# A mixture of experts on one Trainium2 core: the experts' second product with stationary weights and 512 moving tokens

## Chip, core and metric

The kernel runs on one core of one Trainium2 chip. The metric is the device time of one execution in microseconds (us), as the median of several executions. All operands are float32 in memory.

## What is computed

The program runs three stages one after the other, each on the output of the stage before. Cut to what matters:

```python
def _attn_ref(r, k, v, w, u):          # 2 batches, 8 heads, 768 tokens, 48 dimensions
    ...
    for t in range(S):
        cur = np.einsum('bhd,bhe->bhde', u[None] * kt, vt)
        y[:, :, t] = np.einsum('bhd,bhde->bhe', rt, state + cur)
        state = wt[:, :, :, None] * state + np.einsum('bhd,bhe->bhde', kt, vt)

def _moe_ref(x, w_in, w_out):          # x: 1536 x 384, inner width 2048
    h = x @ w_in
    return (h * np.clip(h + 3.0, 0.0, 6.0) / 6.0) @ w_out

def _moe2_ref(x, w_gate, w1, w2):      # 8 experts, inner width 1024
    logits = x @ w_gate
    P = np.exp(logits - logits.max())
    for _ in range(8):
        P /= P.sum(1, keepdims=True) + 1e-09
        P /= P.sum(0, keepdims=True) + 1e-09
        P *= N / E
    out = np.zeros((N, D))
    for e in range(E):
        out += P[:, e:e + 1] * (np.maximum(x @ w1[e], 0.0) @ w2[e])
    return out
```

So every token goes through every expert, and the routing weight P of a token and an expert is one factor on that expert's whole output row.

## The kernel before

Float32 accuracy is kept by splitting each operand of a product into a high and a low part (type fp32r): `parts_of` (line 110) makes `wah`, `wal` and `wbh`, `wbl` of the weights. Each product is then three matmuls: high with high, high with low, low with high.

The program is a list of units, written out in `fast` (line 641). A unit has an upper half (first product and activation) and a lower half (second product), and the lower half runs two units later (`LAG = 2`). Tables of jobs, keyed by unit, put everything else (loads, splits, the routing's normalisation, the input test) between the halves. From the first lower half of the experts on, the order is exactly the order in which the code is written (`manual_schedule`, line 782). Before it, in the first two stages, a scheduler chooses.

The experts are 192 units, one for each expert e (8), block m of 512 tokens (3) and slice f of 128 inner columns (8).

- `ex_up` (line 398): nine matmuls with 128x128 of the expert's first weights as the stationary operand and 512 tokens of `x2h` or `x2l` as the moving one, all into one PSUM tile `ph`. ScalarE makes `hh` (line 410) and VectorE `hl` (line 411), the high and low part of the activated slice: 128 inner columns by 512 tokens.
- `ex_down` (line 414): the second product with the tokens' slice stationary. For each of the 4 groups of 128 tokens, three matmuls: 128x128 of `hh` or `hl` stationary, 384 columns of `wbh` or `wbl` moving, into a PSUM tile `y0` to `y3` of 128 tokens by 384 dimensions, summed over the eight slices f. After slice 7 (a block's end), the sum goes into `acc`, 128 tokens by 384 dimensions each: for expert 0 as a plain copy on ScalarE (line 430), since the routing weights are not ready then. For expert 1 VectorE multiplies `acc` by expert 0's weight (line 433). From expert 1 on it adds `y` times the weight of this expert (line 434). There the weight is one number for each partition, since tokens lie on partitions. After expert 7, `acc` is stored (line 438).
- `acc` lies in the memory of `x2f` (line 540), six tiles of 128 dimensions by 3 by 256 tokens, whose contents are no longer wanted by then.

The four `y` tiles have one buffer each: the first matmul of the next block into `y0` waits until `y0` was read out. PSUM holds 2 tiles `ph`, 4 tiles `y` and 1 for small things (`pss`), of 8 banks.

VectorE executes in the order written: between the `hl` of each unit stand the splits of the next expert's weights (line 114, two 128x768 subtractions every fourth unit), the normalisation of the routing (units 2 to 24 of the experts) and the input test (`flag_stages`, line 441), whose steps load a piece of the inputs into `seen` and look at it. All loads are issued on SyncE's queue (SP) in the order written.

The lines that the prediction's steps touch: matmuls of the first product of the experts L406, of the second L424; their evacuations L410, L411, L430, L433, L434; first and second product of the stage before L274 and L296, where L296 already has weights stationary and 256 tokens moving; transposes on TensorE L253; the subtraction L310 over 128x768 and L283 over 128x256.

Of the kernel before, what the change touches and what calls it, by code (L numbers as in the profile page):

```python
# [8 lines left out]
F32 = mybir.dt.float32  # L9
# [3 lines left out]
AF = mybir.ActivationFunctionType  # L13
ALU = mybir.AluOpType
AX = mybir.AxisListType
PSUM = bass.MemoryType.PSUM

B, H, S, D = 2, 8, 768, 48
DM = H * D
N = B * S  # L20
E = 8
F1 = 2048
FE = 1024
C = 128
NC = S // C
# [18 lines left out]
class Kernel:  # L44
# [269 lines left out]
    def sinkhorn_stages(self):  # L314
# [5 lines left out]
        def gate():  # L320
            gf = pp.tile([128, KT, E], F32, tag="gf", name="gf")
            nc.sync.dma_start(out=gf, in_=self.w_gate.rearrange("(k p) e -> p k e", p=128))
            zero = pp.tile([128, KT, E], F32, tag="gz", name="gz")
            nc.vector.memset(zero, 0.0)
            g = pp.tile([128, KT, 2 * E], F32R, tag="gt", name="gt")
            hi, lo = g[:, :, :E], g[:, :, E:]
            nc.vector.tensor_copy(hi, gf)
            nc.vector.tensor_tensor(out=lo, in0=gf, in1=hi.bitcast(F32), op=ALU.subtract)
            g0 = pp.tile([128, KT, 2 * E], F32R, tag="g0", name="g0")
            nc.vector.tensor_copy(g0[:, :, :E], gf)  # L330
            nc.vector.tensor_copy(g0[:, :, E:], zero)
            q["g"] = g, g0
            q["lt"] = pp.tile([2 * E, N], F32, tag="lt", name="lt")

        def logits(m):
            def go():
# [75 lines left out]
        self.h[e, m, f] = (hh, hl)  # L412

    def ex_down(self, e, m, f):
        nc = self.nc
        bh, bl = self.down_parts(2 + e, f)
        hh, hl = self.h.pop((e, m, f))
        if f == 0:
            self.y = [self.psy.tile([128, 512], F32, tag=f"y{i}", name=f"y{i}") for i in range(4)]
        for i in range(4):  # L420
            o = self.y[i][:, :DM]
            sl = slice(i * 128, (i + 1) * 128)
            for n, (ha, wb) in enumerate(((hh, bh), (hh, bl), (hl, bh))):
                nc.tensor.matmul(o, ha[:, sl], wb, start=f == 0 and n == 0, stop=f == 7 and n == 2)  # L424
        if f == 7:
            for i in range(4):
                t = 4 * m + i
                o, acc = self.y[i][:, :DM], self.acc[t]
                if e == 0:
                    nc.scalar.activation(acc, o, AF.Copy)  # L430
                    continue
                if e == 1:
                    nc.vector.tensor_scalar(out=acc, in0=acc, scalar1=self.pr[:, t, 0:1], scalar2=None, op0=ALU.mult)  # L433
                nc.vector.scalar_tensor_tensor(out=acc, in0=o, scalar=self.pr[:, t, e:e + 1], in1=acc,  # L434
                                               op0=ALU.mult, op1=ALU.add)
                if e == E - 1:
                    c, b = t // 2, t % 2
                    nc.sync.dma_start(out=self.out[b * S + c * C:b * S + (c + 1) * C, :], in_=acc)


    def flag_stages(self):
# [74 lines left out]
    def pool(self, es, name, bufs=1, **kw):  # L516
        return es.enter_context(self.tc.tile_pool(name=name, bufs=bufs, **kw))
# [25 lines left out]
    def slow(self):  # L543
        tc, nc, pool = self.tc, self.nc, self.pool
        self.general = True
        with ExitStack() as top:
            dram = pool(top, "dram", space=bass.MemoryType.DRAM)
            y = dram.tile([DM, B, S], F32, name="y")
            with ExitStack() as es:
                p, q = pool(es, "sa"), pool(es, "sb", 2)  # L550
                ps = pool(es, "sps", 2, space=PSUM)
# [69 lines left out]
            self.hp = pool(top, "hp", 4)  # L621
            self.psy = pool(top, "psy", space=PSUM)
            self.p2 = pool(top, "p2")
            self.pss = pool(top, "pss", space=PSUM)
            self.pr = self.p2.tile([128, N // 128, E], F32, tag="pr", name="pr")
            for st in self.sinkhorn_stages():
                st()
            for e in range(E):
                for i in range(NCH):
                    self.load_chunk(NCH * e + i)  # L630
                    self.split_chunk(NCH * e + i, nc.vector)
                self.lagged([(self.ex_up, self.ex_down, (e, m, f)) for m in range(3) for f in range(8)])

    def lagged(self, units):
        for n in range(len(units) + LAG):
# [5 lines left out]
    def fast(self):  # L641
        tc, nc, pool = self.tc, self.nc, self.pool
        self.general = False
        with ExitStack() as top:
            self.pools(top)
            keep = self.keep
            ph1, ph1x, ph1a = ExitStack(), ExitStack(), ExitStack()
            self.p1 = _Bufs(pool(ph1, "p1", side="right"), {"gh": 3, "gl": 3, "t": 2})
# [40 lines left out]
            def at(n, fn, *args):  # L689
                jobs.setdefault(int(2 * n + 1), []).append((fn, args))  # L690
# [68 lines left out]
            def second():  # L759
                self.x2_parts(NC - 1)  # L760
                ph1.close()
                self.p2 = pool(top, "p2")
                self.pss = pool(top, "pss", space=PSUM)
                self.pr = self.p2.tile([128, N // 128, E], F32, tag="pr", name="pr")
                self.sk = self.sinkhorn_stages()
                self.accumulators()
            at(n1 + LAG - 1, second)
            for s in range(7 + 2 * SK_ITERS):
                at(n1 + LAG + s, lambda s: self.sk[s](), s)

            def flag(x):
                if x == 0:
                    self.fl = self.flag_stages()
                self.fl[x]()
            nst = 2 + 4 * NC * B + 4 * F1 // CH
            lo, hi = n1 + 24, len(units) - 30
            for x in range(nst):
                at(lo + x * (hi - lo) // nst, flag, x)

# [73 lines left out]
```

## Time and profile before

| | |
|---|---|
| median of 3 runs | 1149.19 us (1148.93 to 1149.87) |
| the profiled execution, its own time | 1148.96 us |
| its span in the trace (first to last instruction) | 1147.0 us |
| mean granted TensorE clock | 0.98 of full speed |
| TensorE busy (matmul, weight load) | 97%, 89% of the span |
| VectorE, ScalarE, GpSimd busy | 51%, 28%, 5% |
| DMA traffic | 77.64 MB, mean 68 GB/s |

The profile page gives busy time by engine, the span in 40 slices, the chain of work that ended last, and groups of instructions by line. PE is TensorE's matmul, PEld its weight load, DVE is VectorE, ACT ScalarE, POOL GpSimd and SP SyncE's queue. In the timeline each row is an instruction with its start, its duration, and behind `[` the idle time before it. A matmul's shown duration reaches into the next one's, as matmuls are pipelined: what one costs is read from the start of one to the start of the next.

The experts' part begins at 326 us of the span and ends 6 us before its end.

### The profile page before, as it was taken

The page shows a single profiled execution, that of the slowest core. Times are in us where ns is not written, and L with a number is a line of the kernel's source. Part 1 is how long each engine was busy: PE and PEld are TensorE (multiplying, and loading weights), DVE is VectorE, ACT ScalarE, POOL GpSimd, SP SyncE. Part 2 cuts the span into 40 slices and gives each one's busy share as a digit, 9 for nine tenths or more (in the row PEclk, how much of TensorE's full clock was granted, in tenths as well). Part 3 has the DMA queues.
Part 4 walks back from the last instruction along what each step waited for, and adds up shares of the span by engine and source line. Part 5 has one row for each costly group of instructions (what it writes and reads, how often), then busy time and mean ns, then how long its engine had stood idle before and what let it go on. Part 6 is the DMA issues. An engine that isn't in the chain of part 4 may idle for free.

```text
span 1147.0 us, 15722 instructions
## 1 busy us (share of the span) xinstructions
PE 1112.6 (97%) x6471; PEld 1020.4 (89%) x6471; DVE 583.2 (51%) x1121; ACT 325.7 (28%) x672; POOL 62.4 (5%) x57
## 2 busy tenths in 40 slices
PE   7789989999999999999999999999999999999998
PEld 6678889999998999998999999999999999989997
DVE  8799694535633442554354445345445544532221
ACT  3555554445622222221121122112112211211111
POOL 3443220000000000000000000000000000000000
PEclk7698999999999999999999999999999999999999
DMA  9455330100111001201210220122142124100000
GB/s 293 145 168 183 105 131 2 37 11 1 56 56 36 29 1 44 79 25 52 79 53 25 79 80 25 52 80 89 52 151 74 54 79 137 56 1 1 28 28 31
DMA packets 44208, 77.64 MB, mean 68 GB/s; under 512 B 3296, under 2 KB 26976, under 8 KB 44128
## 3 DMA queue, kind: packets, MB, share of 16 engines
q1 hardware_dynamic: 44128, 76.55, 21.4%
q8 instruction: 53, 0.87, 0.3%
q14 instruction: 27, 0.22, 0.1%
HBM read 74.18 MB, written 2.36 MB: 67 GB/s over the span
## 4 chain that ended last, share of the span: by engine, by line
PE 86%; DVE 9%; DMA 2%; POOL 1%; ACT 1%; issue 1%; SPq 0%; ACTq 0%; DVEq 0%; POOLq 0%
PE y L424 35%; PE ph L406 35%; PE ph L274 7%; PE xa L296 4%; PE xb L296 2%; DMA rkt<-in_tm_dram 1%; DVE x L70 1%; DVE x L71 1%; DVE e L152 1%; DVE gl L283 1%; DVE f L159 1%; PE y L223 1%; DVE x L69 1%; DVE t L279 1%; DMA v<-in_tm_dram 1%
## 5 line engine op out<-in xcount | busy, mean ns | idle before, releaser
L411 DVE SCALAR_TENSOR_TENSOR hl<-ph,hh 128x512 fp32r<-128x512 f32 x192 | 132.7, 691 | 431.0 <-ACT hh L410 430.9
L410 ACT ACTIVATE hh<-ph 128x512 fp32r<-128x512 f32 x192 | 114.6, 597 | 642.9 <-PE ph L406 642.9
L424 PE MATMUL y<-wbh,hl 128*128 128x384 f32 x768 | 259.1, 337 | 0.0
L424 PE MATMUL y<-wbh,hh 128*128 128x384 f32 x768 | 259.0, 337 | 0.0
L424 PE MATMUL y<-wbl,hh 128*128 128x384 f32 x768 | 257.9, 336 | 0.0
L406 PE MATMUL ph<-x2h,wal 128*128 128x512 f32 x576 | 227.8, 396 | 0.0
L406 PE MATMUL ph<-x2l,wah 128*128 128x512 f32 x576 | 227.2, 394 | 0.0
L406 PE MATMUL ph<-x2h,wah 128*128 128x512 f32 x576 | 225.2, 391 | 0.9 <-DVE off L505 0.9
L424 PEld LDWEIGHTS y<-wbh,hh 128*128 128x128 f32 x768 | 144.3, 188 | 8.9 <-DVE x2f L434 0.5
L424 PEld LDWEIGHTS y<-wbl,hh 128*128 128x128 f32 x768 | 144.2, 188 | 8.3
L424 PEld LDWEIGHTS y<-wbh,hl 128*128 128x128 f32 x768 | 144.0, 188 | 0.0
L406 PEld LDWEIGHTS ph<-x2h,wal 128*128 128x128 f32 x576 | 108.0, 187 | 23.3
L406 PEld LDWEIGHTS ph<-x2h,wah 128*128 128x128 f32 x576 | 108.3, 188 | 18.5 <-DVE off L505 0.9
L406 PEld LDWEIGHTS ph<-x2l,wah 128*128 128x128 f32 x576 | 108.1, 188 | 18.2
L274 PE MATMUL ph<-x1h,wah 128*128 128x256 f32 x288 | 84.8, 295 | 3.7 <-DVE t L279 3.7
L274 PE MATMUL ph<-x1h,wal 128*128 128x256 f32 x288 | 81.3, 284 | 1.7 <-DVE wal L114 1.7
L274 PE MATMUL ph<-x1l,wah 128*128 128x256 f32 x288 | 81.9, 285 | 0.0
L277 ACT ACTIVATE t<-ph,three 128x256 f32<-128x256 f32 x96 | 44.5, 470 | 65.1 <-PE ph L274 56.9
L279 DVE SCALAR_TENSOR_TENSOR t<-t,ph 128x256 f32<-128x256 f32 x96 | 39.5, 416 | 44.5 <-ACT t L277 44.4
L296 PE MATMUL xa<-gl,wbh 128*128 128x256 f32 x192 | 56.0, 292 | 6.1 <-DVE gl L283 6.1
L274 PEld LDWEIGHTS ph<-x1h,wah 128*128 128x128 f32 x288 | 55.5, 193 | 6.1 <-DVE t L279 5.1
L274 PEld LDWEIGHTS ph<-x1h,wal 128*128 128x128 f32 x288 | 54.9, 191 | 2.1 <-DVE wal L114 2.1
(125 smaller groups left out, 1309.8 us busy)
## 6 DMA issues: line engine op xcount, KB each, us to landing
stg<-in_w_dram SPq DMA_DIRECT2D x64, 384.0 KB, 4.7
stg<-in_w_in_dram SPq DMA_DIRECT2D x8, 768.0 KB, 6.4
stg<-in_w_out_dram SPq DMA_DIRECT2D x8, 768.0 KB, 4.7
seen<-in_w_in_dram SPq DMA_DIRECT2D x8, 768.0 KB, 4.8
seen<-in_w_out_dram SPq DMA_DIRECT2D x8, 768.0 KB, 4.4
rk<-in_dm_dram SPq DMA_DIRECT2D x12, 448.0 KB, 3.9
seen<-in_dm_dram SPq DMA_DIRECT2D x12, 448.0 KB, 3.8
rkt<-in_tm_dram SPq DMA_DIRECT2D x12, 384.0 KB, 3.9
```

Source lines behind the costliest of these rows:

```text
L69: nc.vector.tensor_scalar(out=x, in0=high, scalar1=3, scalar2=0x3FFFFFF8, op0=ALU.logical_shift_left, op1=ALU.bitwise_and)
L70: nc.vector.scalar_tensor_tensor(out=x, in0=high, scalar=0xC0000000, in1=x, op0=ALU.bitwise_and, op1=ALU.bitwise_or)
L71: nc.vector.scalar_tensor_tensor(out=x, in0=low, scalar=29, in1=x, op0=ALU.logical_shift_right, op1=ALU.bitwise_or)
L152: nc.vector.tensor_tensor_scan(out=e.rearrange("p i t -> p (i t)"), data0=w[:, :WCOL - 1], data1=self.d1e.rearrange("p i t -> p (i t)"), i ...
L274: nc.tensor.matmul(ph, wa[:, kt, :], xa[:, kt, :], start=n == 0, stop=n == 3 * KT - 1)
L277: nc.scalar.activation(t, ph, AF.Relu, bias=self.three)
L279: self.last_u = nc.vector.scalar_tensor_tensor(out=u, in0=t, scalar=6.0, in1=ph, op0=ALU.min, op1=ALU.mult)
L296: nc.tensor.matmul(o, wb[:, kt * 128:(kt + 1) * 128], ga, start=start and n == 0 and kt != 1, stop=stop and n == 2, skip_group_check=True)
L406: nc.tensor.matmul(ph, wa[:, kt, :], xa[:, kt, sl], start=n == 0, stop=n == 3 * KT - 1)
L410: nc.scalar.activation(hh, ph, AF.Relu)
L411: nc.vector.scalar_tensor_tensor(out=hl, in0=ph, scalar=0.0, in1=hh.bitcast(F32), op0=ALU.max, op1=ALU.subtract)
L424: nc.tensor.matmul(o, ha[:, sl], wb, start=f == 0 and n == 0, stop=f == 7 and n == 2)
```

## The change

`ex_down` is turned round for all blocks but the last (expert 7, block 2). For each of three groups of 128 model dimensions, `wbh` or `wbl` (128x128) is stationary and the 512 tokens of `hh` or `hl` move, into `y0`, `y1` and `y2`, each 128 dimensions by 512 tokens. The sums are kept by model dimension, in `x2f`'s own layout (`accumulate`). A routing weight is now one number for each column, so the weights have to stand as a row, the same on all 128 partitions: `keep_routing` transposes the finished `pr` and writes it to DRAM (`pd`), and `spread_routing` loads one expert's 1536 weights onto all partitions (`pb`, 128x1536). `weigh_first` multiplies expert 0's sums by its weights. From expert 1 on, VectorE multiplies `y` by `pb` into `p` (128x512) and adds the two halves of `p` to the two tiles of `x2f`.

The output wants tokens on partitions: `turn` transposes one chunk of 256 tokens back (six 128x128 transposes on TensorE, two copies on ScalarE into `acc`), and `store` writes it. Chunks 4 and 5 are turned during expert 7's first block, before the last block, which still works by token, adds to them. Chunks 0 to 3 are finished and stored while the last block runs. `pss` gets a second buffer, so that all 8 PSUM banks are in use. The input test starts 12 units later (36 instead of 24 units into the experts) and ends at the same unit.

The diff, without the slow path that runs only if the input test fails, and without line changes that follow from it:

```diff
@@ -412,30 +412,86 @@
         self.h[e, m, f] = (hh, hl)
 
     def ex_down(self, e, m, f):
         nc = self.nc
         bh, bl = self.down_parts(2 + e, f)
         hh, hl = self.h.pop((e, m, f))
+        by_token = (e, m) == (E - 1, 2)
         if f == 0:
-            self.y = [self.psy.tile([128, 512], F32, tag=f"y{i}", name=f"y{i}") for i in range(4)]
-        for i in range(4):
-            o = self.y[i][:, :DM]
+            self.y = [self.psy.tile([128, 512], F32, tag=f"y{i}", name=f"y{i}") for i in range(4 if by_token else KT)]
+        for i, y in enumerate(self.y):
             sl = slice(i * 128, (i + 1) * 128)
-            for n, (ha, wb) in enumerate(((hh, bh), (hh, bl), (hl, bh))):
-                nc.tensor.matmul(o, ha[:, sl], wb, start=f == 0 and n == 0, stop=f == 7 and n == 2)
+            for n, (wb, ha) in enumerate(((bh, hh), (bl, hh), (bh, hl))):
+                go = dict(start=f == 0 and n == 0, stop=f == 7 and n == 2)
+                if by_token:
+                    nc.tensor.matmul(y[:, :DM], ha[:, sl], wb, **go)
+                else:
+                    nc.tensor.matmul(y, wb[:, sl], ha, **go)
         if f == 7:
-            for i in range(4):
-                t = 4 * m + i
-                o, acc = self.y[i][:, :DM], self.acc[t]
-                if e == 0:
-                    nc.scalar.activation(acc, o, AF.Copy)
-                    continue
-                if e == 1:
-                    nc.vector.tensor_scalar(out=acc, in0=acc, scalar1=self.pr[:, t, 0:1], scalar2=None, op0=ALU.mult)
-                nc.vector.scalar_tensor_tensor(out=acc, in0=o, scalar=self.pr[:, t, e:e + 1], in1=acc,
-                                               op0=ALU.mult, op1=ALU.add)
-                if e == E - 1:
-                    c, b = t // 2, t % 2
-                    nc.sync.dma_start(out=self.out[b * S + c * C:b * S + (c + 1) * C, :], in_=acc)
+            for i, y in enumerate(self.y):
+                if by_token:
+                    t = 4 * m + i
+                    nc.vector.scalar_tensor_tensor(out=self.acc[t], in0=y[:, :DM], scalar=self.pr[:, t, e:e + 1],
+                                                   in1=self.acc[t], op0=ALU.mult, op1=ALU.add)
+                    self.store(t)
+                else:
+                    self.accumulate(e, m, i, y)
+    def accumulate(self, e, m, i, y):
+        nc = self.nc
+        halves = [(self.x2f[2 * m + s][:, i, :], slice(s * NB1, (s + 1) * NB1)) for s in range(2)]
+        if e == 0:
+            for x, s in halves:
+                nc.scalar.activation(x, y[:, s], AF.Copy)
+            return
+        p = self.tmp.tile([128, KT * CH], F32, tag="x", name="p")[:, :512]
+        nc.vector.tensor_tensor(out=p, in0=y, in1=self.pb[:, m * 512:(m + 1) * 512], op=ALU.mult)
+        for x, s in halves:
+            nc.vector.tensor_tensor(out=x, in0=x, in1=p[:, s], op=ALU.add)
+    def store(self, t):
+        c, b = t // 2, t % 2
+        self.nc.sync.dma_start(out=self.out[b * S + c * C:b * S + (c + 1) * C, :], in_=self.acc[t])
+    def keep_routing(self):
+        nc, pp = self.nc, self.p2
+        NT = N // 128
+        pe = pp.tile([128, E, NT], F32, tag="lg", name="pe")
+        nc.vector.tensor_copy(pe, self.pr.rearrange("p t e -> p e t"))
+        ps = self.pss.tile([E * NT, 128], F32, tag="s", name="pt")
+        nc.tensor.transpose(ps, pe.rearrange("p e t -> p (e t)"), self.ident)
+        pt = pp.tile([128, N], F32, tag="lt", name="pt")[:E * NT, :128]
+        nc.vector.tensor_copy(pt, ps)
+        nc.sync.dma_start(out=self.pd, in_=pt)
+    def spread_routing(self, e):
+        tag = "lt" if e else "seen"
+        self.pb = self.p2.tile([128, N], F32, tag=tag, name="pb")
+        row = self.pd.rearrange("(e t) p -> e (t p)", e=E)[e:e + 1, :]
+        self.nc.sync.dma_start(out=self.pb, in_=row.to_broadcast([128, N]))
+    def weigh_first(self, c, pb):
+        x = self.x2f[c]
+        w = pb[:, c * NB1:(c + 1) * NB1].unsqueeze(1).to_broadcast([128, KT, NB1])
+        self.nc.vector.tensor_tensor(out=x, in0=x, in1=w, op=ALU.mult)
+    def turn(self, c):
+        nc, x = self.nc, self.x2f[c]
+        ps = []
+        for b in range(B):
+            ps.append(self.pss.tile([128, KT, 128], F32, tag="s", name="tr"))
+            for k in range(KT):
+                nc.tensor.transpose(ps[b][:, k, :], x[:, k, b * C:(b + 1) * C], self.ident)
+        for b in range(B):
+            nc.scalar.activation(self.acc[2 * c + b], ps[b].rearrange("p k t -> p (k t)"), AF.Copy)
+    def finish_chunk(self, c):
+        self.turn(c)
+        for b in range(B):
+            self.store(2 * c + b)
 
 
     def flag_stages(self):
...
@@ -760,7 +832,7 @@
                 self.x2_parts(NC - 1)
                 ph1.close()
                 self.p2 = pool(top, "p2")
-                self.pss = pool(top, "pss", space=PSUM)
+                self.pss = pool(top, "pss", 2, space=PSUM)
                 self.pr = self.p2.tile([128, N // 128, E], F32, tag="pr", name="pr")
                 self.sk = self.sinkhorn_stages()
                 self.accumulators()
@@ -768,12 +840,30 @@
             for s in range(7 + 2 * SK_ITERS):
                 at(n1 + LAG + s, lambda s: self.sk[s](), s)
 
+            q = {}
+
+            def spread(e):
+                self.spread_routing(e)
+                q[e] = self.pb
+            r1 = n1 + LAG + 7 + 2 * SK_ITERS
+            at(r1, self.keep_routing)
+            at(r1, spread, 0)
+            at(r1 + 1, spread, 1)
+            for c in range(NC):
+                at(r1 + 3 + c // 2, lambda c: self.weigh_first(c, q[0]), c)
+            for e in range(2, E):
+                at(n1 + 24 * e + LAG, spread, e)
+            for c in range(4, NC):
+                at(len(units) - 24 + LAG + 2 * c - 6, self.turn, c)
+            for c in range(4):
+                at(len(units) - 24 + 8 * (c // 2 + 1) + LAG + c % 2, self.finish_chunk, c)
+
             def flag(x):
                 if x == 0:
                     self.fl = self.flag_stages()
                 self.fl[x]()
             nst = 2 + 4 * NC * B + 4 * F1 // CH
-            lo, hi = n1 + 24, len(units) - 30
+            lo, hi = n1 + 36, len(units) - 30
             for x in range(nst):
                 at(lo + x * (hi - lo) // nst, flag, x)
```

How the change moves instructions, at three places. First TensorE in the middle of a block of expert 1 or 2, one lower half (`y0` to `y3` are PSUM tiles, `wbh` and `wbl` the second weights' parts, `hh` and `hl` the tokens' slice; the second name right of the arrow is the stationary operand in the rows before and after alike, the first the moving one). Before:

```order
L424 MATMUL y0_5076<-wbh_4269,hh_5122 128x384
L424 MATMUL y0_5076<-wbl_4270,hh_5122 128x384
L424 MATMUL y0_5076<-wbh_4269,hl_5123 128x384
L424 MATMUL y1_5077<-wbh_4269,hh_5122 128x384
L424 MATMUL y1_5077<-wbl_4270,hh_5122 128x384
L424 MATMUL y1_5077<-wbh_4269,hl_5123 128x384
L424 MATMUL y2_5078<-wbh_4269,hh_5122 128x384
L424 MATMUL y2_5078<-wbl_4270,hh_5122 128x384
L424 MATMUL y2_5078<-wbh_4269,hl_5123 128x384
L424 MATMUL y3_5079<-wbh_4269,hh_5122 128x384
L424 MATMUL y3_5079<-wbl_4270,hh_5122 128x384
L424 MATMUL y3_5079<-wbh_4269,hl_5123 128x384
```

Now:

```order
L406 MATMUL ph_5245<-x2h_2998,wal_4242 128x512
L429 MATMUL y0_5216<-hh_5177,wbh_4099 128x512
L429 MATMUL y0_5216<-hh_5177,wbl_4100 128x512
L429 MATMUL y0_5216<-hl_5178,wbh_4099 128x512
L429 MATMUL y1_5217<-hh_5177,wbh_4099 128x512
L429 MATMUL y1_5217<-hh_5177,wbl_4100 128x512
L429 MATMUL y1_5217<-hl_5178,wbh_4099 128x512
L429 MATMUL y2_5218<-hh_5177,wbh_4099 128x512
L429 MATMUL y2_5218<-hh_5177,wbl_4100 128x512
L429 MATMUL y2_5218<-hl_5178,wbh_4099 128x512
L406 MATMUL ph_5270<-x2h_2998,wah_4372 128x512
```

Twelve matmuls of 384 columns became nine of 512, 4608 columns either way, and the order of upper and lower halves is the same.

Second, VectorE at a block's end from expert 2 on. Before (the rows with `seen`, `m`, `tt` and `ok` are a look of the input test):

```order
L411 SCALAR_TENSOR_TENSOR hl_5820<-ph_5809,hh_5819 128x512
L434 SCALAR_TENSOR_TENSOR x2f0_804<-y0_5601,pr_3933,x2f0_804 128x384
L434 SCALAR_TENSOR_TENSOR x2f0_804<-y1_5602,pr_3933,x2f0_804 128x384
L434 SCALAR_TENSOR_TENSOR x2f1_1110<-y2_5603,pr_3933,x2f1_1110 128x384
L434 SCALAR_TENSOR_TENSOR x2f1_1110<-y3_5604,pr_3933,x2f1_1110 128x384
L462 TENSOR_REDUCE m_5839<-seen_5781 112x1
L463 TENSOR_REDUCE m_5839<-seen_5781 112x1
L471 TENSOR_SCALAR tt_5842<-m_5839 112x1
L472 TENSOR_TENSOR ok_4772<-ok_4772,tt_5842 112x1
L471 TENSOR_SCALAR tt_5845<-m_5839 112x1
L472 TENSOR_TENSOR ok_4772<-ok_4772,tt_5845 112x1
L411 SCALAR_TENSOR_TENSOR hl_5859<-ph_5848,hh_5858 128x512
```

Now:

```order
L411 SCALAR_TENSOR_TENSOR hl_6147<-ph_6136,hh_6146 128x512
L448 TENSOR_TENSOR p_6159<-y0_5947,pb_5471 128x512
L450 TENSOR_TENSOR x2f4_3461<-x2f4_3461,p_6159 128x256
L450 TENSOR_TENSOR x2f5_3923<-x2f5_3923,p_6159 128x256
L448 TENSOR_TENSOR p_6163<-y1_5948,pb_5471 128x512
L450 TENSOR_TENSOR x2f4_3461<-x2f4_3461,p_6163 128x256
L450 TENSOR_TENSOR x2f5_3923<-x2f5_3923,p_6163 128x256
L448 TENSOR_TENSOR p_6167<-y2_5949,pb_5471 128x512
L450 TENSOR_TENSOR x2f4_3461<-x2f4_3461,p_6167 128x256
L450 TENSOR_TENSOR x2f5_3923<-x2f5_3923,p_6167 128x256
L411 SCALAR_TENSOR_TENSOR hl_6182<-ph_6171,hh_6181 128x512
```

The four L434 became nine instructions. Only the three L448 read PSUM, so only they free a `y` tile.

Third, TensorE in expert 7, where chunk 5 is turned back between a lower and an upper half (before, `ph` follows `y3` there directly):

```order
L429 MATMUL y2_9149<-hh_9194,wbl_8808 128x512
L429 MATMUL y2_9149<-hl_9195,wbh_8807 128x512
L487 MATMUL tr_9263<-ident_160,x2f5_3923 128x128 x3
L487 MATMUL tr_9267<-ident_160,x2f5_3923 128x128 x3
L406 MATMUL ph_9273<-x2h_2998,wah_8952 128x512
```

Six transposes were put in. There are six such places, one for each chunk. Up to the first lower half of the experts nothing moved on any engine.

## Rows read from the trace of the kernel before

**Rows 1.** The profile page: span, busy time of the engines.

```profile
span 1147.0 us, 15722 instructions
PE 1112.6 (97%) x6471; PEld 1020.4 (89%) x6471; DVE 583.2 (51%) x1121; ACT 325.7 (28%) x672; POOL 62.4 (5%) x57
```

**Rows 2.** Windows: busy us and counts by engine, granted clock, DMA share, GB/s.

```profile
786.20:819.50 33.30, 33.30 (x169) 30.20 (x168) 20.43 (x40) 7.71 (x12) 0.00 (x0) 1.00 0.29 95
```

**Rows 3.** Timeline, PE: first matmuls of halves, then one twenty units later.

```profile
700.34 0.39 PE L406 MATMUL ph<-x2h,wah 128*128 128x512 f32 x1
...
702.42 0.33 PE L424 MATMUL y<-wbh,hh 128*128 128x384 f32 x1
...
704.53 0.39 PE L406 MATMUL ph<-x2h,wah 128*128 128x512 f32 x1
...
784.07 0.39 PE L406 MATMUL ph<-x2h,wah 128*128 128x512 f32 x1
```

**Rows 4.** Timeline, PE, the last two lower halves, with no upper half before.

```profile
1136.98 0.33 PE L424 MATMUL y<-wbh,hh 128*128 128x384 f32 x1
...
1139.06 0.33 PE L424 MATMUL y<-wbh,hh 128*128 128x384 f32 x1
```

**Rows 5.** Timeline, PE, one lower half of the stage before.

```profile
249.16 0.28 PE L296 MATMUL xa<-gh,wbh 128*128 128x256 f32 x1
...
250.22 0.28 PE L274 MATMUL ph<-x1h,wah 128*128 128x256 f32 x1
```

**Rows 6.** Timeline, PE, three transposes of 128x128 between matmuls of 256 columns.

```profile
98.15 0.28 PE L296 MATMUL xb<-gh,wbh 128*128 128x256 f32 x1
98.27 0.49 PE L253 MATMUL xp<-ident,ys 128*128 128x128 f32 x3
98.51 0.36 PE L274 MATMUL ph<-x1h,wah 128*128 128x256 f32 x1
98.72 0.28 PE L274 MATMUL ph<-x1l,wah 128*128 128x256 f32 x1
```

**Rows 7.** Timeline, PE, from a block's end of expert 1 into the next block.

```profile
505.40 0.33 PE L424 MATMUL y<-wbh,hh 128*128 128x384 f32 x1
...
511.00 0.34 PE L424 MATMUL y<-wbh,hl 128*128 128x384 f32 x1
511.20 0.44 PE L424 MATMUL y<-wbh,hh 128*128 128x384 f32 x1
511.47 0.33 PE L424 MATMUL y<-wbl,hh 128*128 128x384 f32 x1
```

**Rows 8.** Timeline, DVE, the same stretch.

```profile
506.23 0.69 DVE L411 SCALAR_TENSOR_TENSOR hl<-ph,hh 128x512 fp32r<-128x512 f32 x1 [1.67 <-ACT hh L410]
506.84 0.41 DVE L433 TENSOR_SCALAR x2f<-x2f,pr 128x384 f32<-128x384 f32 x1
507.36 0.62 DVE L434 SCALAR_TENSOR_TENSOR x2f<-y,pr,x2f 128x384 f32<-128x384 f32 x1
507.90 0.41 DVE L433 TENSOR_SCALAR x2f<-x2f,pr 128x384 f32<-128x384 f32 x1
...
510.52 0.62 DVE L434 SCALAR_TENSOR_TENSOR x2f<-y,pr,x2f 128x384 f32<-128x384 f32 x1
```

**Rows 9.** Groups by line and form: count, busy us and mean ns, idle before.

```profile
L411 DVE SCALAR_TENSOR_TENSOR hl<-ph,hh 128x512 fp32r<-128x512 f32 x192 | 132.7, 691 | 431.0 <-ACT hh L410 430.9
...
L283 DVE TENSOR_TENSOR gl<-t,gh 128x256 fp32r<-128x256 f32 x96 | 42.6, 453 | 23.2 <-ACT gh L282 22.9
...
L430 ACT ACTIVATE x2f<-y 128x384 f32<-128x384 f32 x12 | 5.9, 492 | 0.3
L310 DVE TENSOR_TENSOR x2l<-x2f,x2h 128x768 fp32r<-128x768 f32 x6 | 5.6, 956 | 1.8 <-ACT x2h L309 1.8
```

**Rows 10.** Who waited for L434: us, times.

```profile
PEld y L424: 0.5, 3
```

**Rows 11.** DMA issues: KB of one, median us from issue to landing.

```profile
seen<-in_w_in_dram SPq DMA_DIRECT2D x8, 768.0 KB, 4.8
```

More of the change, by code (lines that the diff above doesn't have):

```diff
@@ L332, in gate @@
             q["g"] = g, g0
-            q["lt"] = pp.tile([2 * E, N], F32, tag="lt", name="lt")
+            q["lt"] = pp.tile([128, N], F32, tag="lt", name="lt")[:2 * E]
         def logits(m):
@@ L548, in slow @@
             y = dram.tile([DM, B, S], F32, name="y")
+            self.pd = dram.tile([E * N // 128, 128], F32, name="pd")
             with ExitStack() as es:
@@ L631, in slow @@
                     self.split_chunk(NCH * e + i, nc.vector)
-                self.lagged([(self.ex_up, self.ex_down, (e, m, f)) for m in range(3) for f in range(8)])
+                for m in range(3):
+                    if e == E - 1 and m == 2:
+                        for c in range(2 * m):
+                            self.finish_chunk(c)
+                    self.lagged([(self.ex_up, self.ex_down, (e, m, f)) for f in range(8)])
+                if e == 0:
+                    self.keep_routing()
+                    self.spread_routing(0)
+                    for c in range(NC):
+                        self.weigh_first(c, self.pb)
+                if e == E - 2:
+                    for c in range(4, NC):
+                        self.turn(c)
+                if e < E - 1:
+                    self.spread_routing(e + 1)
     def lagged(self, units):
@@ L645, in fast @@
             self.pools(top)
+            self.pd = pool(top, "dram", space=bass.MemoryType.DRAM).tile([E * N // 128, 128], F32, name="pd")
             keep = self.keep
@@ L762, in second @@
                 self.p2 = pool(top, "p2")
-                self.pss = pool(top, "pss", space=PSUM)
+                self.pss = pool(top, "pss", 2, space=PSUM)
                 self.pr = self.p2.tile([128, N // 128, E], F32, tag="pr", name="pr")
@@ L769, in fast @@
                 at(n1 + LAG + s, lambda s: self.sk[s](), s)
+            q = {}
[6 more added lines that the diff above has]
+            at(r1 + 1, spread, 1)
+            for c in range(NC):
+                at(r1 + 3 + c // 2, lambda c: self.weigh_first(c, q[0]), c)
+            for e in range(2, E):
+                at(n1 + 24 * e + LAG, spread, e)
+            for c in range(4, NC):
+                at(len(units) - 24 + LAG + 2 * c - 6, self.turn, c)
+            for c in range(4):
+                at(len(units) - 24 + 8 * (c // 2 + 1) + LAG + c % 2, self.finish_chunk, c)
             def flag(x):
```

## The prediction, made before the changed kernel ran

> **What bounds the kernel now.** I read the page first [rows 1]: TensorE is busy for 97% of the span, VectorE for half of it. A busy TensorE proves little by itself, since matmuls are pipelined, so next come the windows. In a stretch of 33.3 us in the experts' part in which VectorE does more than in its neighbours (20.43 us), TensorE has no gap at the full granted clock of 1.00 [rows 2]. So in this part, some 815 us of the span, the time is the number of matmuls times the distance from one start to the next. VectorE, ScalarE and the loads matter only where they make TensorE wait.
>
> Then the timeline, for these distances. An upper half (nine matmuls of 512 columns) lasts from 700.34 to 702.42 us, 2.08 us; the lower half after it (twelve of 384) to 704.53, 2.11 us. Twenty units later the upper half starts at 784.07, so a unit takes 83.73 / 20 = 4.187 us [rows 3]. The two halves have the same 4608 columns, and yet differ by 0.027 us. Where that comes from is seen at the end, where two lower halves follow each other without an upper half between: there one takes 1139.06 - 1136.98 = 2.08 us, 173.3 ns a matmul [rows 4]. Nine matmuls of 512 in 2.08 us are 231.1 ns each. Both are 0.4514 ns a column: **the price is by column, with nothing to be seen for a matmul as such**. The 0.027 us arise only where a half of 384 columns follows a half of 512. In the stage before, where lower and upper half both have 256 columns and weights are stationary in both, a lower half takes 1.06 us for nine matmuls, 118 ns each, with no such loss [rows 5].
>
> **The change part by part.**
>
> *The matmuls.* 184 lower halves (192 less the eight of the last block) go from twelve matmuls of 384 to nine of 512. By the price by column nothing is saved. What goes is the loss behind the upper half: a unit becomes 2 x 2.08 = 4.16 instead of 4.187 us, 0.027 x 184 = 5.0 us less. The bounds are nothing, if the loss belongs to the lower half for another reason, and 5.0 us. I take 5.0, because a lower half of equal width shows no loss [rows 5].
>
> *A wait that goes.* At expert 1's block ends VectorE runs a multiplication and an addition for each of four tiles [rows 8], and frees `y3` at 511.14 (510.52 + 0.62). TensorE's first matmul into it starts at 511.20 instead of 511.17, and the one after 0.27 instead of 0.17 us later [rows 7], 0.13 us in all. Three such waits are in the trace, 0.5 us by the weight loads [rows 10]; I take 0.3 us off. These multiplications are now six of 128x768 by a row, before the first addition; the nearest row has 0.956 us each [rows 9], two to a unit of 4.16 us, beside TensorE.
>
> *The transposes.* Six groups of six are added on TensorE, and they lie on the path, as it has no gap. Three transposes of 128x128 took from 98.27 to 98.51, and the matmul behind them 0.21 instead of 0.12 us to the next start: 0.24 + 0.09 = 0.33 us [rows 6]. Six cost at most 0.66 us, six groups 4.0 us; below that, 0.57 us a group (3.4 us) if the loss behind them falls once. One more transpose for the routing weights: 0.1 us. TensorE waits for none of them: chunks 4 and 5 have been complete for three units, chunk 0 is turned one unit after its last addition, and the copy of the routing weights that the single transpose needs stands right behind one `hl`, which ends 0.7 us before the lower half does.
>
> The Trainium skill speaks against this step. By "TensorE: Matmul & The Clock Gate", section on PE-mode transpose, one 128x128 transpose takes about 275 ns in a kernel; an estimate from it is 36 x 0.275 = 9.9 us, and the sum would end at +4.7 us. The trace does not agree, since the second and third transpose of a group are about 0.1 us apart [rows 6].
>
> *VectorE at a block's end.* This is the cover to check. Count from the start of the block's last lower half, 505.40 in the rows. `hl` starts 0.83 us later and the next instruction at 1.44 [rows 7, 8]. The multiplication of `y0` by the row (128x512, like `hl`, 0.69 us [rows 9]) ends at 2.13. The first addition needs its result; the row of a dependent pair shows 0.11 us from end to start (506.84 + 0.41 to 507.36 [rows 8]). An addition of 128x256 is at most 0.453 us [rows 9] and overlaps its successor by about 0.08, as `hl` does (0.69 long, 0.61 to the next start [rows 8]). So a tile takes 0.69 + 0.11 + 0.35 + 0.35 = 1.5 us, and `y2` is free at 1.44 + 2 x 1.5 + 0.69 = 5.13. TensorE wants it after this lower half, an upper half and two thirds of the next lower half: 2.08 + 2.08 + 1.39 = 5.55. It fits, with 0.4 us to spare; `y0` and `y1` have over 1 us. Queued behind this on VectorE is the next `hl`, about 1 us late, whose reader comes two units later. A look of the input test ahead of that `hl` of the block end would have to last over 3.5 us to delay it. For expert 0 six copies on ScalarE replace four of 0.492 us [rows 9]; at that price they take 3.0 us and end well before 5.55.
>
> *The loads.* Eight loads of 128x1536 (768 KB) go on SP's queue; the nearest one lands after 4.8 us [rows 11]. Each waits until the expert before has been added and holds back the chunk loads and test loads behind it by some us. A chunk is split four units (17 us) after its issue, and the row is first read seven units after its own. Only the first is closer: `pd` written, then read, then `weigh_first` three units (12.5 us) after the transpose. If it were late, VectorE would wait, and the `hl` behind has over 4 us. I cost this at nothing.
>
> *The end.* The last block is by token as before, with the same four additions and stores.
>
> **Sum** against the profiled execution: -5.0 - 0.3 + 4.0 + 0.1 = -1.2 us, 1148.96 to 1147.8. The median of the runs shown is 0.23 us above that execution, so I say **1148.0 us**.
>
> **The rivals.**
>
> *A: the loss stays with the lower half* (slower). The 0.027 us could come from ScalarE reading `ph` during its first half, which was so in each of the 192 units and is not so at the end [rows 4]. Against it: in the stage before ScalarE reads `ph` in the same place, without loss [rows 5]. It decides if a turned lower half takes 2.11 us. Then the matmuls give nothing: 1149.19 - 0.3 + 4.1 = 1153.0 us. The Trainium skill has a rule that lies between: by "TensorE: Matmul & The Clock Gate", section "Back-to-back issue gap", a lone matmul costs N / 2.4 + 2.5 ns, an estimate of 1.950 us for twelve and 1.942 us for nine, 1.4 us in all and the sum at +2.4. The trace disagrees with both durations (2.08).
>
> *B: TensorE waits for `y2`* (slower). If a tile's three instructions on VectorE take over 1.71 us ((5.55 - 0.69 - 1.44) / 2) instead of 1.5, `y2` is late at each of the 20 block ends from expert 1 on that have this form. With both additions at their full 0.453 and each waiting 0.11 for the one before, a tile takes 1.93, and `y2` is late by 0.44: 20 x 0.44 = 8.8, so 1156.8 us. For it: 0.4 us is little. Against: the two additions don't depend on each other, and independent neighbours overlap [rows 8].
>
> *C: a matmul has a price of its own* (faster). A line through 118 ns at 256 and 231.1 at 512 columns [rows 3, 5] leaves 4.9 ns a matmul. There are 552 fewer: 2.7 us more, 1145.3 us. Against it: 384 columns would take 174.6 by that line, and take 173.3 [rows 4]. The same section of the Trainium skill also gives 81 ns for 128 and 131 ns for 512 columns in a long stream; an estimate from these is 0.19 us saved in a lower half, 35 us in all. Nine matmuls of 512 in 2.08 us [rows 3] speak against it.
>
> **How the numbers follow.** My forecast has 0.70, A 0.14, B 0.08, C 0.08. 0.2% of the time, 2.3 us, is about what a measurement can tell from no change: below 1146.9 is faster, above 1151.5 slower. The forecast's own range is 1147.2 (transposes cheaper by 0.6) to 1150.5 (half of the 5.0 us not given), all within 0.2%. The range reaches to A, and on the other side a third of the way to C: 1146.6 to 1153.2; B and most of C stay out, 0.16. Chances: faster 0.08, same 0.72 (A in part would fall here too), slower 0.20.
>
> **What would show it.** In the changed profile, right: lower halves of 2.08 us, units of 4.16; TensorE without gaps at block ends; groups of transposes of about 0.6 us; the L448 to L450 chains 1.5 us a tile. A shows as lower halves of 2.11; B as waits of `y` on L448; C as distances under 231 ns. The forecast is wrong if the turned matmuls are not paced like those of the upper half, or if VectorE or the loads make TensorE wait where I cost them at nothing.

## The result, and the profile after

| | median us (lowest to highest) | against the kernel before |
|---|---|---|
| before | 1149.10 (1148.93 to 1149.87) | |
| the changed kernel | 1134.27 (1133.67 to 1135.73) | ratio 0.9872, 95% interval 0.9854 to 0.9889 |

The change is faster by 1.3%, 14.8 us; 1148.0 us with a range from 1146.6 to 1153.2 was forecast. Both the size and "about the same" were wrong. The profiled execution took 1133.67 us; its span is 15.4 us shorter than before.

The profile page of the changed kernel, answering to [rows 1]:

```profile
span 1131.6 us, 14831 instructions
PE 1098.3 (97%) x5956; PEld 949.0 (84%) x5956; DVE 621.1 (55%) x1217; ACT 331.4 (29%) x690; POOL 63.1 (6%) x57
```

TensorE is still what sets the end, and VectorE has 38 us more to do. The gain stands in TensorE's timeline of the changed kernel, the stretch that answers to [rows 3] (start, duration, engine, line, operation):

```profile
703.52 0.39 PE L406 MATMUL ph<-x2h,wah 128*128 128x512 f32 x1
...
705.56 0.39 PE L429 MATMUL y<-hh,wbh 128*128 128x512 f32 x1
...
707.60 0.39 PE L406 MATMUL ph<-x2h,wah 128*128 128x512 f32 x1
...
785.12 0.39 PE L406 MATMUL ph<-x2h,wah 128*128 128x512 f32 x1
```

A unit takes (785.12 - 703.52) / 20 = 4.080 us instead of 4.187. The turned lower half takes 2.04 us. But so does the **upper half, which nobody touched**: 2.04 instead of 2.08 us, with the same instructions and operands. Each of the 18 matmuls is 226.7 ns from the next. So 231.1 ns for 512 columns, on which the forecast's price rested, was not the price of a matmul of 512 columns; it was that price with a loss on top.

The ledger: 0.107 us less in each of 184 units is 19.7 us. The transposes took back 4.1 us (shown below), and some smaller terms are added up under "What is left". The experts' part, from its first to its last matmul, went from 814.9 us (326.07 to 1140.97) to 799.9 (325.62 to 1125.54), 15.0 us less; the stage before ended 0.4 us earlier, without a change in its instructions.

### The profile page after: what moved, and what is told of

Read it like the earlier page. It is cut to its first block, busy times and chain, and to the rows that moved or that the text cites. A ratio compares the mean times of both kernels' runs of the same rounds, so it can differ in the third digit from the quotient of the medians.

```text
span 1131.6 us, 14831 instructions
## 1 busy us (share of the span) xinstructions
PE 1098.3 (97%) x5956; PEld 949.0 (84%) x5956; DVE 621.1 (55%) x1217; ACT 331.4 (29%) x690; POOL 63.1 (6%) x57
## 4 chain that ended last, share of the span: by engine, by line
PE 87%; DVE 7%; DMA 2%; ACT 1%; POOL 1%; issue 1%; SPq 0%; ACTq 0%; DVEq 0%; POOLq 0%
PE ph L406 35%; PE y L429 33%; PE ph L274 7%; PE xa L296 5%; PE xb L296 2%; PE y L427 1%; DMA rkt<-in_tm_dram 1%; DVE x L70 1%; PE y L223 1%; DVE x L71 1%; DMA v<-in_tm_dram 1%; DVE gl L283 1%; PE y L219 1%; DVE e L152 1%; ACT dv L185 1%
## 5 line engine op out<-in xcount | busy, mean ns | idle before, releaser
L406 PE MATMUL ph<-x2h,wal 128*128 128x512 f32 x576 | 224.6, 390 | 0.0
L406 PE MATMUL ph<-x2l,wah 128*128 128x512 f32 x576 | 224.4, 390 | 0.0
L429 PE MATMUL y<-hl,wbh 128*128 128x512 f32 x552 | 215.0, 389 | 0.0
L429 PE MATMUL y<-hh,wbh 128*128 128x512 f32 x552 | 214.9, 389 | 0.0
L429 PE MATMUL y<-hh,wbl 128*128 128x512 f32 x552 | 214.9, 389 | 0.0
L429 PEld LDWEIGHTS y<-hh,wbl 128*128 128x128 f32 x552 | 103.7, 188 | 21.5
L429 PEld LDWEIGHTS y<-hl,wbh 128*128 128x128 f32 x552 | 103.7, 188 | 21.5
L429 PEld LDWEIGHTS y<-hh,wbh 128*128 128x128 f32 x552 | 103.7, 188 | 21.5
```

The source lines that it names most:

```text
L406: nc.tensor.matmul(ph, wa[:, kt, :], xa[:, kt, sl], start=n == 0, stop=n == 3 * KT - 1)
L429: nc.tensor.matmul(y, wb[:, sl], ha, **go)
```

## The experiments

After the result there were two theories. **W**: a matmul costs its columns and about 13 ns, and a further loss follows each change of the moving width; turning removed both three matmuls and the change of width. **T**: the loss belongs to the form with the tokens' slices stationary, whatever the widths.

**Equal widths without turning.** The kernel before, with blocks of 384 tokens:

```diff
+TB = 384
...
-        sl = slice(m * 512, (m + 1) * 512)
+        sl = slice(m * TB, (m + 1) * TB)
...
-        for i in range(4):
+        for i in range(TB // 128):
```

> The kernel before with blocks of 384 tokens instead of 512 (four blocks, 256 units instead of 192): tokens' slices stay the stationary operand of the second product, and all matmuls of the experts are 384 columns wide. Theory W (a matmul costs its columns plus about 13 ns, and where halves of 512 and of 384 columns follow each other each unit of two halves loses a further 0.067 us): units of 18 x 173.3 ns = 3.12 us, 256 of them 798.7 us against 192 x 4.187 = 803.9 before, so about 1144 us. Theory T (the loss belongs to the form with the tokens' slices stationary, whatever the widths): units of about 3.19 us, 256 of them 816 us, so about 1161 us.

Measured: 1145.76 us (ratio 0.9972, interval 0.996 to 0.9983). TensorE's timeline of this run, first matmuls of an upper half, its lower half, and an upper half twenty units later:

```profile
690.45 0.33 PE L408 MATMUL ph<-x2h,wah 128*128 128x384 f32 x1
...
692.01 0.33 PE L426 MATMUL y<-wbh,hh 128*128 128x384 f32 x1
...
752.85 0.34 PE L408 MATMUL ph<-x2h,wah 128*128 128x384 f32 x1
```

Both halves take 1.56 us, a unit 62.40 / 20 = 3.120, 173.3 ns a matmul, with no loss (the granted clock was 1.00 here and in the stretches of the other runs that are compared below, but for one that is named there). T falls: here tokens' slices are stationary, and nothing is lost. The run is 3 to 4 us faster than before although it issues 576 more matmuls (256 x 18 against 192 x 21).

**The same matmuls, half the changes of width.** The kernel before, two upper halves and then two lower halves:

```diff
-                if n < len(units):
+                pair = n >= n1 + LAG and (n - n1) % 2 == 0
+                if n < len(units) and not (n > n1 + LAG and not pair and (n - n1) % 2):
                     units[n][0](*units[n][2])
...
+                if pair and n + 1 < len(units):
+                    units[n + 1][0](*units[n + 1][2])
```

> The kernel before with two upper halves followed by two lower halves, so that the width changes once in a unit instead of twice; same matmuls. W with the loss paid at each change of width: half of 0.067 us a unit goes, units of 4.153 us on average, about 6.4 us less, 1143 us. If the loss belongs to any stream that holds both widths, or to the token form (T): units stay at 4.187 us, 1149 us.

Measured: 1141.88 us (ratio 0.9937, interval 0.992 to 0.9955). Its timeline, the first matmuls of the first upper half, of the second, of the two lower halves (of the first lower half the seventh as well), of the next upper half, and of an upper half forty units after the first:

```profile
704.13 0.39 PE L406 MATMUL ph<-x2h,wah 128*128 128x512 f32 x1
...
706.21 0.39 PE L406 MATMUL ph<-x2h,wah 128*128 128x512 f32 x1
...
708.25 0.33 PE L424 MATMUL y<-wbh,hh 128*128 128x384 f32 x1
...
709.32 0.33 PE L424 MATMUL y<-wbh,hh 128*128 128x384 f32 x1
...
710.36 0.33 PE L424 MATMUL y<-wbh,hh 128*128 128x384 f32 x1
...
712.44 0.39 PE L406 MATMUL ph<-x2h,wah 128*128 128x512 f32 x1
...
870.26 0.39 PE L406 MATMUL ph<-x2h,wah 128*128 128x512 f32 x1
```

The first half after a change is slow and the second is not: 2.08 and then 2.04 us at 512 columns, 2.11 and then 2.08 at 384. Two units take 8.31 us, and over forty a unit is (870.26 - 704.13) / 40 = 4.153 us, as W said. So the loss is paid at each change: about 0.04 us over the nine matmuls of 512 that follow, 0.026 over the first six of those of 384 (1.07 us to 709.32, and 1.04 for the next six), together the 0.067 of a unit before. The time fell by somewhat more than the 6.4 us of the sum. The experts' part itself went from 814.9 to 808.3 us, 6.6 less; the stage before ended 1.4 us earlier in this trace (324.70 against 326.07), which the change does not touch.

**A change at every matmul, and its control.** The matmuls of an upper and a lower half taken in turn, in the kernel before and in the changed one (the matmuls of a lower half are queued, `take` issues them one by one, and a block's `y` is read out behind the upper half):

```diff
+    def take(self, n):
+        for _ in range(min(n, len(self.queued))):
+            self.queued.pop(0)()
...
                 nc.tensor.matmul(ph, wa[:, kt, :], xa[:, kt, sl], start=n == 0, stop=n == 3 * KT - 1)
                 n += 1
+                self.take(1 if n < 3 * KT else 99)
```

> The kernel before with the matmuls of an upper and a lower half taken in turn, so that the width changes some 17 times in a unit instead of twice; same matmuls, sums and operands. W with the loss paid at each change: units clearly longer than 4.187 us, up to 8 times 0.067 us more (4.7 us), the whole up to 100 us slower. T, or a loss that does not depend on changes: units of 4.187 us, about 1149 us.

> The changed kernel with the matmuls of an upper and a lower half taken in turn, all 512 wide (the last block apart): the control for taking them in turn as such. W: units stay at 4.08 us, about 1134 us. If it is the change of PSUM tile or of operand from one matmul to the next that costs, units grow here as they do in the mixed run of the kernel before.

Measured: 1159.25 and 1145.22 us, one execution each. First the timeline of the run with 512 and 384 in turn, then that of its control with 512 alone:

```profile
700.74 0.40 PE L410 MATMUL ph<-x2l,wah 128*128 128x512 f32 x1
700.98 0.34 PE L432 MATMUL y<-wbl,hh 128*128 128x384 f32 x1
701.16 0.40 PE L410 MATMUL ph<-x2h,wal 128*128 128x512 f32 x1
701.39 0.34 PE L432 MATMUL y<-wbh,hl 128*128 128x384 f32 x1
701.57 0.40 PE L410 MATMUL ph<-x2h,wah 128*128 128x512 f32 x1
```

```profile
700.13 0.39 PE L410 MATMUL ph<-x2h,wah 128*128 128x512 f32 x1
700.35 0.39 PE L437 MATMUL y<-hh,wbh 128*128 128x512 f32 x1
700.58 0.39 PE L410 MATMUL ph<-x2l,wah 128*128 128x512 f32 x1
700.81 0.39 PE L437 MATMUL y<-hh,wbl 128*128 128x512 f32 x1
701.03 0.39 PE L410 MATMUL ph<-x2h,wal 128*128 128x512 f32 x1
```

With two widths a pair takes 0.413 us (over the whole run the median is 413 ns) against 226.7 + 173.3 = 400 for the two prices. With one width, two matmuls take 0.45 us, 2 x 226.7, although the PSUM tile, the operands and the kind of half change each time. So it is the width, and neither the tile nor the operand. The size was over-expected: a unit takes 4.240 us (median) where the two prices give 4.120, so 17 changes cost 0.12 us, not 8 times 0.067. Nor is it the loss of the longer streams, cut short by the next change. In the pairs the first matmul after a change hardly loses (229 ns at 512 columns and 171 at 384 on average, together the 400 of the two prices), and the loss lies on those behind it. Here each 512 takes 237 ns and each 384 takes 176. What the loss is made of stays open.

The control's total is 11 us above the changed kernel, not by its price but by waits. By the lengths of its units, some 6 us lie at the first matmuls of five blocks, which want a free `y` sooner when the halves are taken in turn, as rival B had it. Another 4 us lie around the transpose of the routing weights, which waits for its operand. Two lines of the control's list of waits (in total, times, longest):

```profile
PE y L437 <- DVE p L465: 3.5, 5, 0.9
...
PE pt L480 <- DVE pe L478: 2.1, 1, 2.1
```

More than these 2.1 us is lost there: behind the wait the granted clock was 0.50 for a stretch, the lower of its two levels, and matmuls of 512 are 427 ns apart in it. The window (the last three numbers are granted clock, DMA share and GB/s), and two matmuls of the timeline, six apart:

```profile
441.80:445.20 3.40, 3.40 (x10) 2.63 (x9) 0.00 (x0) 0.00 (x0) 0.00 (x0) 0.50 0.18 36
```

```profile
442.06 0.63 PE L437 MATMUL y<-hl,wbh 128*128 128x512 f32 x1
...
444.62 0.63 PE L437 MATMUL y<-hl,wbh 128*128 128x512 f32 x1
```

**The price of a matmul.** The changed kernel with its matmuls cut into two of 256 columns, first only in the lower halves (the edit shown), then in both:

```diff
-                    nc.tensor.matmul(y, wb[:, sl], ha, **go)
+                    for s in range(2):
+                        nc.tensor.matmul(y[:, s * 256:(s + 1) * 256], wb[:, sl], ha[:, s * 256:(s + 1) * 256],
+                                         start=go["start"] and s == 0, stop=go["stop"], skip_group_check=True)
```

> The changed kernel with each matmul of a turned lower half cut into two of 256 columns, upper halves left at 512: eighteen of 256 follow nine of 512. W (a price of its own for each matmul, and a loss after each change of width): a lower half of 18 x 118 ns = 2.12 us instead of 2.04, and a loss after the changes that brings the upper half back from 2.04 towards 2.08 us; units of 4.2 us or more, about 1156 us. Price alone, no loss from widths: units of 4.16 us, about 1149 us. Price by column alone: units of 4.08 us, 1134 us.

> The changed kernel with all matmuls of both halves cut into two of 256 columns (the last block's lower halves stay at 384): equal widths, but twice as many matmuls. W: no loss, 36 x 118 ns = 4.24 us a unit instead of 4.08, about 30 us slower, 1164 us. Price by column alone: 1134 us. If weights that stay the same from one matmul to the next made the second cheaper: less than 4.24 us a unit.

Measured: 1159.69 and 1177.62 us, one execution each. The timelines, first of the run with 512 and 256, where the last row is twenty units after the first:

```profile
694.91 0.40 PE L406 MATMUL ph<-x2h,wah 128*128 128x512 f32 x1
...
696.98 0.40 PE L430 MATMUL y<-hh,wbh 128*128 128x256 f32 x2
...
779.31 0.40 PE L406 MATMUL ph<-x2h,wah 128*128 128x512 f32 x1
```

and of the run with 256 alone, two upper halves twenty units apart:

```profile
694.33 0.28 PE L408 MATMUL ph<-x2h,wah 128*128 128x256 f32 x1
...
780.73 0.28 PE L408 MATMUL ph<-x2h,wah 128*128 128x256 f32 x1
```

With 256 alone a unit takes 86.40 / 20 = 4.320 us, 120.0 ns a matmul: 0.240 us more than with 512 for 18 more matmuls, 13.3 ns each. Each of these matmuls has a weight load of its own, as in all the streams here. A matmul takes 2 ns more than the 118 that both expectations took from the stage before, so this run came out nearly 14 us slower than W said. With 512 and 256 the upper half is back at 2.07 us and the unit takes (779.31 - 694.91) / 20 = 4.22, where equal-width prices give 9 x 226.7 + 18 x 120 = 4.20: a loss again, but a third of that between 512 and 384. This run also parts the width from the role of the operands: here both halves have weights stationary and the widths differ, with a loss; in the run of 384 columns the roles differ and the widths don't, without one.

Three streams of equal width thus give 120.0, 173.3 and 226.7 ns for 256, 384 and 512 columns: 53.3 ns for each 128 columns, and **13.3 ns for each matmul**. The Trainium skill, "TensorE: Matmul & The Clock Gate", section "Back-to-back issue gap", has N / 2.4 + 2.5 ns: the slope agrees with these runs (128 / 2.4 = 53.3), the constant does not.

**The transposes.** The changed kernel without them:

```diff
...
-            for k in range(KT):
-                nc.tensor.transpose(ps[b][:, k, :], x[:, k, b * C:(b + 1) * C], self.ident)
-        for b in range(B):
-            nc.scalar.activation(self.acc[2 * c + b], ps[b].rearrange("p k t -> p (k t)"), AF.Copy)
...
```

> The changed kernel without turning the chunks back: no transposes and no copies after them, chunks 0 to 3 are stored as they lie, by model dimension, and the last block adds to chunks 4 and 5 as they lie. Prices the transposes: by the trace of the changed kernel six groups of 0.57 us and 0.12 us at the matmul behind each, 4.1 us less, about 1130 us. If they were covered by something: 1134 us.

Measured: 1128.18 us, one execution. First and last matmul of the experts' part in its timeline:

```profile
324.66 0.39 PE L406 MATMUL ph<-x2h,wah 128*128 128x512 f32 x1
...
1120.50 0.34 PE L427 MATMUL y<-wbh,hl 128*128 128x384 f32 x1
```

That is 795.8 us against 799.9 with the transposes: 4.1 us, 0.68 a group, all on the path. The profiled executions differ by 5.5 us; outside this part, the stage before ended 1.0 us earlier. In the changed kernel a group reads

```profile
1039.34 0.82 PE L487 MATMUL tr<-ident,x2f 128*128 128x128 f32 x6
1039.92 0.48 PE L406 MATMUL ph<-x2h,wah 128*128 128x512 f32 x1
1040.23 0.39 PE L406 MATMUL ph<-x2l,wah 128*128 128x512 f32 x1
1040.46 0.39 PE L406 MATMUL ph<-x2h,wal 128*128 128x512 f32 x1
1040.69 0.40 PE L406 MATMUL ph<-x2h,wah 128*128 128x512 f32 x1
1040.93 0.39 PE L406 MATMUL ph<-x2l,wah 128*128 128x512 f32 x1
```

0.58 us for six, 0.08 us more than its usual 0.23 at the next start, and then 0.23 to 0.24 again where the units around have 0.227. Transposes have 128 columns, so this fits a change of width; but they are also float32 where the matmuls around are fp32r, and no run parts the two.

**Both kernels' order by two.** The changed kernel with two upper and then two lower halves, the edit of the pairs above:

> The changed kernel with two upper halves followed by two lower halves: the control for the same order in the kernel before. W: nothing to win where all widths are equal, units of 4.08 us on average, 1134 us (0.3 us less in the last block, which still has both widths). If the order by two saves by itself (longer distance to the readers of hh, fewer switches between the halves' operands): 6 us or so less, as in the kernel before.

Measured: 1132.34 us, one execution. In its timeline two units take 8.160 us:

```profile
698.40 0.39 PE L406 MATMUL ph<-x2h,wah 128*128 128x512 f32 x1
...
861.60 0.39 PE L406 MATMUL ph<-x2h,wah 128*128 128x512 f32 x1
```

163.20 us for forty units, 4.080 each, no change. The one time was 2 us lower; 1.0 us of that lies ahead of the experts' part, which starts at 324.60 us here and at 325.62 in the changed kernel. So it was timed beside the changed kernel:

> The changed kernel as it is, beside the next one on the same chip. By the sums from the traces, 0.107 us less in each of 184 units and 4.1 us for the transposes, 15 to 16 us under the kernel before: 1133 to 1135 us.

> The changed kernel with two upper halves followed by two lower halves, now timed. W: only the last block has both widths, so 0.3 us at most is to be had: the same as the changed kernel within the noise, and an interval against it that holds 1. If the order by two helps otherwise (it took 1132.3 us in one look): 2 us less than the changed kernel.

Measured: 1134.19 us for the changed kernel (ratio to before 0.9871, interval 0.9854 to 0.9887) and 1133.42 us by two (0.9864, 0.9847 to 0.988). The intervals overlap almost wholly. The order by two gained 7 us where widths differ and nothing that the times can tell where they are equal, so it did not save by itself. In the traces the experts' part is 0.2 us shorter by two (799.7 us against 799.9, in both pairs of traces), about what W expects of the last block. No version here beats the changed kernel clearly.

## Why the prediction was wrong

**The failed step** is the first term of the sum, "By the price by column nothing is saved", and before it "the price is by column, with nothing to be seen for a matmul as such". It compared 173.3 ns for 384 columns, from the only stretch of the experts where halves of equal width follow each other [rows 4], with 231.1 ns for 512, from a stretch where both halves pay for the change of width [rows 3]. The two gave the same price for a column by chance: 13.3 ns a matmul weigh more on 384 columns, and the loss, unseen in the upper half, made up for it on 512. The term was put at -5.0 us and is -19.7: 3 matmuls x 13.3 ns = 0.040 us and the whole loss of 0.067 us in each of 184 units, 7.4 and 12.3 us. Of the loss the forecast saw only the 0.027 us in the lower half. The turned matmuls are paced like those of the upper half, as it wanted; what it had wrong was the pace of the upper half.

Rows that spoke against the step stood in the forecast. Rival C drew a line through 256 and 512 columns and found 4.9 ns a matmul; it was set aside because 384 columns did not lie on it, when that misfit was the sign that the three durations were not from like streams. With 226.7 in place of 231.1 the same line leaves 9.3 ns a matmul. C was priced for its matmuls only, at 2.7 us, and so even its 1145.3 us was 11 us too slow. Its sign, distances under 231 ns, is what the trace shows.

**A** (the loss stays with the lower half) fell in the result itself: the turned lower half lost it, with ScalarE reading `ph` at the same place, 0.20 us into the half that starts at 705.56 (before, at 702.62 in a half that starts at 702.42). ScalarE's timeline of the changed kernel:

```profile
705.76 0.60 ACT L410 ACTIVATE hh<-ph 128x512 fp32r<-128x512 f32 x1 [2.01 <-PE ph L406]
```

**B** did not come about. This is VectorE's timeline of the changed kernel at a block's end, whose last lower half starts at 762.68; it answers to [rows 8]:

```profile
763.51 0.69 DVE L411 SCALAR_TENSOR_TENSOR hl<-ph,hh 128x512 fp32r<-128x512 f32 x1 [3.39 <-ACT hh L410]
764.12 0.68 DVE L448 TENSOR_TENSOR p<-y,pb 128x512 f32<-128x512 f32 x1
764.83 0.76 DVE L450 TENSOR_TENSOR x2f<-x2f,p 128x256 f32<-128x256 f32 x2
765.51 0.68 DVE L448 TENSOR_TENSOR p<-y,pb 128x512 f32<-128x512 f32 x1
...
766.91 0.68 DVE L448 TENSOR_TENSOR p<-y,pb 128x512 f32<-128x512 f32 x1
```

The chain starts 1.44 us into the lower half, as worked out; a tile takes 1.39 us where 1.5 was put, and `y2` is free at 4.91 where 5.13 was put. TensorE wants it at 2.04 + 2.04 + 1.36 = 5.44. So the cover was sized rightly, with 0.5 us to spare, and the control taken in turn shows waits for `y` where it is shorter.

**The transposes** were right: 4.0 us forecast, 4.1 measured, and the 275 ns each of the Trainium skill ("TensorE: Matmul & The Clock Gate", section on PE-mode transpose) would have been more than twice that. The transpose of the routing weights cost about 0.15 us where 0.1 was put. **The loads** hide as costed; `pb` lands after 4.2 us, and no wait on it is in the trace.

**What is left.** 19.7 - 4.1 is 15.6 us, and the experts' part lost 15.0. The waits at expert 1's block ends were rightly foreseen: the three units behind them took 4.31 to 4.33 us before and take 4.08 now, 0.4 us in all beyond the 0.107 of each, where 0.3 was forecast. So 1.0 us is missing, and 0.7 of it is in expert 0, where small matmuls of the routing's normalisation stand between the halves in every second unit. From its first matmul to the first of expert 1 it took 105.7 us before (326.07 to 431.79) and takes 104.1 now (325.62 to 429.73). That is 1.6 us less, where 22 units at 0.107 give 2.3. Another 0.2 us is in the three units behind that, with the last of the normalisation and the transpose of the routing weights. The changed kernel's timeline there:

```profile
374.74 0.28 PE L385 MATMUL cp<-cs,ones 128*128 128x8 f32 x2
374.88 0.48 PE L406 MATMUL ph<-x2h,wah 128*128 128x512 f32 x1
375.19 0.40 PE L406 MATMUL ph<-x2l,wah 128*128 128x512 f32 x1
375.42 0.40 PE L406 MATMUL ph<-x2h,wal 128*128 128x512 f32 x1
375.66 0.40 PE L406 MATMUL ph<-x2h,wah 128*128 128x512 f32 x1
```

Behind 8 columns the matmuls of 512 are 0.23 to 0.24 us apart again, a loss that turning does not remove. It fits a change of width, but as with the transposes these matmuls are float32, and no run parts width from type.

## What to carry to other kernels

Read the price of a matmul from streams of one width, and never set a duration from a mixed stream against one from a pure stream; where one operand shape is to change, look whether its neighbours' durations hang on it. Where TensorE has no gaps, equal and wide moving operands are worth a change of layout: here three matmuls fewer in a unit and one width for all gave 1.7% of the time, of which transposes took back 0.4. If a width can't be changed, put matmuls of the same width next to each other: two and two instead of one and one got 7 of these 15 us without touching a shape.

## What was not expected of the hardware

A matmul of one width slows down those of another width that follow it: with 384 columns before, nine matmuls of 512 lost 41 ns in all, the tenth none; with 512 before, the first six of 384 lost 26 ns. Between 512 and 256 a unit lost 20 ns. It follows the width of the moving operand: changing PSUM tile, operands or half at every matmul cost nothing where the width stayed. Why is open; no run looked inside it. At a granted clock of 0.50 matmuls of 512 were 427 ns apart, less than twice the 226.7 at 1.00. Open too is why 256 columns take 118 ns in the stage before [rows 5] and 120 in the experts.
